# Two pairs of heads per turning transfer, and a new order of the work, in a linear attention with a maxout feed-forward layer

## The chip, the cores and the metric

The kernel runs on one core of a Trainium2 chip. The metric is the device time of one execution in microseconds, and lower is better. Five engines work side by side, each through its own instructions in order: PE (TensorE, matrix products; its loads of weights are listed as PEld), DVE (VectorE), ACT (ScalarE), POOL (GpSimd) and SP (SyncE, which here only issues DMA transfers). Engines wait for each other by semaphores.

## The reference

```
q_s = exp(q - max(q, -1));   q_s /= sum(q_s, -1) + 1e-9      # q, k, v: 8 batches, 8 heads, 576 rows, 64 wide
k_s = exp(k - max(k, 2));    k_s /= sum(k_s, 2) + 1e-9       # over the rows
kv  = einsum('bhsd,bhse->bhde', k_s, v)                      # 64 x 64 for each head
x   = einsum('bhsd,bhde->bhse', q_s, kv) -> (8 * 576, 8 * 64)
h   = maximum(maximum(x @ w1, x @ w2), x @ w3)               # 512 -> 768, float64 weights
out = h @ w_out                                              # 768 -> 512, float32
```

## The kernel before

The unit of the attention is a pair of heads of one batch, since two heads of 64 fill the 128 partitions. Pair n is batch n // 4 and heads 2 (n % 4) and the next; there are 32 pairs. The feed-forward layer runs over chunks of 512 rows, one for each batch, and a ninth of the 8 x 64 rows that are left over. Its products are in two float32r terms each for operand and weights (a high and a low part, three matmuls for one). The weights come as 64-bit words, which `Slice` joins to float32 and splits, 24 slices in all: bits of them are put together by DVE, ACT and POOL (`wx`, `wst`, `wf`), and the parts land in `wa` (three gates, 18 slices) and `oh`, `ol` (second product, six).

The stages: in the first 31 us loads, the first pairs and the first slices; then chunks 0, 1 and 2 by plain products (the gates, L946, and the second product, L993), with the attention of batches 0 to 4 between them; from 292 us on the other six chunks in three "duos" by seven products instead of eight (L1174, of tiles `ws` that SyncE loads back from DRAM copies `keep_a` and `keep_s`), with the attention of batches 5 to 7 between them. Batches 0 and 1 are "turned": PE transposes keys and queries against `ident` (L559, L578, L799). Pair 1's sums are taken by PE after its product (L812, L813), DVE divides (L820), and PE transposes the result (L837, `xr`). The other 24 pairs, n = 8 to 31, are "plain", and the change concerns mostly these:

- keys: loads into `kt` (L515, and L517 for the rows left over), maxima by DVE and POOL, `ksub` (L603), exponentials by ACT (L610); after every second pair `two_products` multiplies the keys' and values' tiles of both (L626), DVE inverts the sums (L632), and ACT and DVE write the head matrices `bdh` and `bdl`, high and low (L639, L647).
- queries: load into `qt` (L548), maximum by DVE (L725), then either nine exponentials with sums by ACT (L729, for n from 8 to 20) or a difference by DVE (L735), one exponential by ACT (L744) and a sum by DVE (L746). The division is by nine ACT instructions (L755, n from 8 to 23) or one of DVE (L760). DVE transposes blocks of 32 into `tb` (L764), and eight DMA transfers (L777) put these blocks in their places in `qT`, which has two rooms.
- query product, `x_steps` (L851): for n from 8 to 16 (`by_f32`) plain float32 matmuls of `qT` with `bdf2`, in two halves; for the others `qT` is split into `q_h` by ACT (L786) and `q_l` by DVE (L789), and six float32r matmuls follow. ACT and DVE copy the result to `x` or `xf`, from where the chunk's products read it.

Nothing of the order is left to the hardware. Generators yield a `Step` for each instruction or small group; `Streams` is a planner that gives every step a cost, due times (`AT`, `FIRST`, `CHUNK`, `PAIR_STEP` and the like set the ranks), rooms of buffers, and picks step by step what each engine does next. Its times are only a plan: on the chip each engine goes through the list that came out, and waits where something is late. SyncE's list matters as the others do: it issues in order, at most eight transfers are open at a time, and a transfer that waits holds up those behind it.

Of the kernel before, what the change touches and what calls it, by code (L numbers as in the profile page):

```python
# [8 lines left out]
F32 = mybir.dt.float32  # L9
# [17 lines left out]
DMA_BEGINS, DMA_LANDS, DMA_EACH, DMA_KB, DMA_LANES = 0.25, 1.3, 0.0095, 0.0375, 8  # L27
DMA_MORE = 1.2
WAIT = 0.02

COLD = 34.0, 1.85

EAGER = 0.21

FIRST, CHUNK, SLICE = 115.59, 38.94, 2.04

PAIR_STEP, LATE_STEP = 7.34, 0.49

AT = (236.9, -68.4, 25.0, -23.0, 44.8, 76.9, 350.7, 199.3)
STEP = (0, 1.04)  # L40
SLICES_AT, SLICE_STEP, SLICE_HI, SLICE_LO = -80.12, -0.08, -2.09, -1.75
GATES_AT = 1000.0
FIRST_LOADS = 'vkwkKqvVwkwqKVqvkvwq'
# [4 lines left out]
Q_BY_ACT = (0, 3, 4, 5, 7)  # L48
# [15 lines left out]
LEFT_AT, KEEP_AT, PLAIN_AT, MIX_AT, MIX_STEP = 149.21, 133.44, 71.96, 363.56, -36.84  # L64
# [26 lines left out]
class Step:  # L91
# [3 lines left out]
    def __init__(self, engine, cost, after=(), gives=None, take=(), free=(), port="", kb=None, rank=None):  # L95
        self.engine, self.gives, self.take, self.free, self.port, self.kb = engine, gives, take, free, port, kb
        self.cost = cost if isinstance(cost, tuple) else (cost,) * len(engine)
        self.after, self.rank = after, rank


class Streams:
# [123 lines left out]
def linear_attention_then_maxout_ffn(  # L225
# [91 lines left out]
    tb = place("tb", [P, 2, BL * QS], F32, SCR_AT + 4608)  # L317
    half = place("kh", [P, 2, 2, D], F32, SCR_AT + 6912)
# [14 lines left out]
    kbuf = [const.tile([P, 2, 5, D], F32, name=f"kt{i}") for i in range(2)]  # L333
    vbuf = [const.tile([P, 2, 5, NV], F32, name=f"vt{i}") for i in range(2)]
    bdh, bdl, bdf2 = [], [], []
# [49 lines left out]
    st = Streams({"pf": 4, "pa": BANKS[0], "sm": BANKS[1], "keT": 1, "hp": NJ, "tmp": 3, "ke": 2, "kep": 1, "qe": 2, "qf": 1, "qt": 2, "tb": 1, "qT": 2, "qhl": 1, "wf": 4, "ws": len(ws), "hs": 2}, {"pf": in_pf, "ws": in_ws, "tb": list(range(TURNED * NP, B * NP))})  # L385
    turn_pools = []

# [87 lines left out]
    class Pair:  # L475
# [30 lines left out]
        def k_load(self):  # L506
            if self.b:
                prev = self.ago("ksub") if self.n >= NP + 2 else None
                if self.turned:
                    for hh in range(2):  # L510
                        yield Step("S", 0.65, [prev], kb=(512, 256))
                        nc.sync.dma_start(out=self.kt[:, 0:4, hh, :], in_=head_rows(k, self.b, 2 * self.g + hh))
                else:
                    yield Step("S", 0.5, [prev], kb=(256, 1024))
                    nc.sync.dma_start(out=self.kt[:, :, 0:4, :], in_=main_rows(k, self.b, self.hs))  # L515
                yield Step("S", 0.69, gives=("k", self.n), kb=(128, 256))
                nc.sync.dma_start(  # L517
                    out=self.kt[0:LEFT, 4] if self.turned else self.kt[0:LEFT, :, 4, :], in_=left_rows(k, self.b, self.hs)
                )

        def v_load(self):
            if self.b:
# [5 lines left out]
                for hh in range(2):  # L528
                    e = yield Step("S" if self.turned else V_ON, 0.5 if self.turned else 0.63, [prev], kb=(128, 1024) if self.turned else (512, 256))
                    if not self.turned:  # L530
                        self.vt = vbuf[self.n % 4]
                    (nc.sync if e == "S" else nc.scalar).dma_start(out=self.vt[:, hh, 0:4, 0:D], in_=head_rows(v, self.b, 2 * self.g + hh))
                yield Step("S", 0.68, gives=("v", self.n), kb=(128, 256))
# [3 lines left out]
        def q_load(self):  # L537
# [7 lines left out]
            else:  # L545
                yield Step("S", 0.5, ["wo"], gives=("q", self.n), take=[("qt", self.n)], kb=(128, 2304))
# [39 lines left out]
        def k_plain(self):  # L586
            n, kt = self.n, self.kt
            yield Step("V", dve(256) + dve(128) * 2, ["turn", ("k", n), ("kmt", n - 1) if n > TURNED * NP else None], port="V")
# [10 lines left out]
            if n % 2:  # L599
                ke = self.ke = turn_pools[0].tile([P, 5, 2, D], F32, name="kep", bufs=1)  # L600
            else:
                ke = self.ke = att.tile([P, 5, 2, D], F32, name="ke")
# [11 lines left out]
        def two_products(self):  # L614
# [5 lines left out]
                free=[("ke", n - 1), ("kep", n)], gives=("kv", n),  # L620
# [13 lines left out]
            for i, p in enumerate(both):  # L634
                fine = by_f32(p.n)
                last = [] if i == 0 else room
                yield Step("A", 0.65, gives=("bd", p.n) if fine else None, free=last if fine else ())
                for r in heads:
                    nc.scalar.activation(  # L639
                        out=(bdf2 if fine else bdh)[p.m][r, r], in_=kv[r, i * P : i * P + D], func=AF.Copy,  # L640
                        scale=rk[r, i : i + 1],
                    )
                if fine:
                    continue
# [39 lines left out]
        def q_steps(self):  # L684
# [79 lines left out]
            nc.vector.transpose(  # L764
                out=tb.rearrange("p e (c s) -> p s e c", s=QS), in_=self.qt.rearrange("p s (e c) -> p s e c", e=2)
            )
            for i in range(P // BL):
                for e in range(2):
                    end = i == P // BL - 1 and e == 1
                    eng = yield Step(  # L770
                        TB_ON, 0.6, ["turn"], take=[("qT", n)] if i == e == 0 else (), free=[("tb", n)] if end else (),
                        gives=("qhl" if by_f32(n) else "qT", n) if end else None, kb=(32, 1152),
                    )
# [3 lines left out]
                    (nc.sync if eng == "S" else nc.scalar).dma_start(  # L777
                        out=self.qT[r : r + BL, BL * QS * (i % 2) : BL * QS * (i % 2 + 1)],
                        in_=tb[BL * i : BL * (i + 1), e, :],
                    )  # L780
# [5 lines left out]
            nc.scalar.copy(out=q_h, in_=self.qT)  # L786
            yield Step("V", dve(S), free=[("qT", n)], gives=("qhl", n), port="V")
            q_l = turn_pools[0].tile([P, S], F32R, name="q_l", bufs=1)
# [35 lines left out]
        def x_steps(self):  # L824
# [3 lines left out]
            fine = by_f32(n)  # L828
# [4 lines left out]
            yield Step("T", cost, after, take=[room] if self.turned else [room, small], gives=("xmm", n), free=[] if after_sums else [freed])  # L833
# [46 lines left out]
    def left_queries():  # L880
# [24 lines left out]
        yield Step("T", 0.5, take=room, free=[("qt", "left")])  # L905
# [5 lines left out]
        yield Step("A", act(CH), take=[("qT", "left")], free=room)  # L911
        qT = turn_pools[0].tile([P, S], F32, name="qT", bufs=2)
# [121 lines left out]
    def keep_weights():  # L1034
# [3 lines left out]
        for i in range(3):  # L1038
            for c in range(NC):
                e = yield Step(  # L1040
                    KEEP_ON, 0.6, [last, *(("split", 3 * j + i) for j in range(NJ))], gives=("kept", i, c), kb=(128, 6144)
                )
                (nc.sync if e == "S" else nc.scalar).dma_start(out=keep_a[i][:, c], in_=wa[i][:, c].bitcast(F32))
# [274 lines left out]
    def open_turn():  # L1318
# [6 lines left out]
        for i in range(4):  # L1325
            nc.gpsimd.memset(vbuf[i][:, :, :, D:NV], 1.0)
            nc.gpsimd.memset(vbuf[i][LEFT:P, :, 4, :], 0.0)
        mixes.append(turn_pools[0].tile([P, 2, NC, 2, P], F32, name="mix"))
        for name, to in (("bdf", bdf2), ("bdh", bdh), ("bdl", bdl)):
            for i in range(2):  # L1330
                to.append(turn_pools[0].tile([P, P], F32 if name == "bdf" else F32R, name=f"{name}{i}"))
# [43 lines left out]
    for (b, g), p in pairs.items():  # L1375
# [11 lines left out]
        st.add(p.q_steps(), at + 0.2, step)  # L1387
        if p.turned:
# [64 lines left out]
```

## Time and profile before

| what | value |
|---|---|
| median of three runs | 680.42 us (680.39 to 680.74) |
| the profiled execution | 681.24 us, its span 679.5 us |
| PE, DVE, ACT, POOL busy | 641.8, 441.0, 365.1, 57.4 us |
| mean granted clock of PE | 0.994 |
| DMA | 135.97 MB in 148534 packets |

The span runs from the first to the last instruction. Busy time is the time in which an engine has an instruction in work. In the rows of waits, the engine that waited and the tile and line that it waited with stand ahead of the arrow, and what came last behind it. "SPq" is SyncE's queue of DMA issues: the time there is that of the issue, not of the transfer. Line numbers in rows of the profile are those of the kernel before; in the changed kernel L777 is L781, L851 is L857, L837 is L843, L626 is L624, L755 is gone.

### The profile page before, as it was taken

Reading aid. Unit: us, or ns where it says so; the run is one execution under the profiler, and the core shown is the slowest. Engines: PE = TensorE matmul, PEld = TensorE weight load, DVE = VectorE, ACT = ScalarE, POOL = GpSimd, SP = SyncE. Lnnn points to the kernel's source line nnn. Section 1 sums busy time; section 2 is a strip of 40 time slices with the busy share of each in tenths; the row PEclk is TensorE's granted clock in tenths of the full one; section 3 lists DMA queues with packets and bytes.
Section 4 is the critical chain, followed back from the end, with each engine's and each line's share of the span. In section 5 each row is a group of like instructions: output and inputs, shape, how many; then the busy total and the mean of one; then the engine's idle time right before and its main releaser. Section 6 shows DMA issues by size and latency. Waiting matters only on the chain.

```text
span 679.5 us, 10529 instructions
## 1 busy us (share of the span) xinstructions
PE 641.8 (94%) x3362; PEld 516.9 (76%) x3362; DVE 441.0 (65%) x830; ACT 365.1 (54%) x1031; POOL 57.4 (8%) x74
## 2 busy tenths in 40 slices
PE   2799999999999899899999999999999999999997
PEld 1587877777777677788888777777888788888875
DVE  6999999476845767997767889945335912333521
ACT  5889759636898786684624365633233532123132
POOL 2232344110000001000000010000000000000000
PEclk9989999999999999999999999999999999999999
DMA  9969587876566667899998756465665126666121
GB/s 234 327 200 326 179 263 238 293 228 157 148 180 172 199 195 201 250 284 322 298 320 259 219 158 173 150 181 174 198 190 173 75 84 194 190 198 189 60 63 62
DMA packets 148534, 135.97 MB, mean 200 GB/s; under 512 B 52992, under 2 KB 120064, under 8 KB 147328
## 3 DMA queue, kind: packets, MB, share of 16 engines
q1 hardware_dynamic: 148400, 135.18, 65.7%
q8 instruction: 27, 0.44, 0.3%
q14 instruction: 27, 0.22, 0.1%
q10 hardware_dynamic: 80, 0.13, 0.1%
HBM read 95.16 MB, written 33.03 MB: 189 GB/s over the span
## 4 chain that ended last, share of the span: by engine, by line
PE 70%; DMA 11%; DVE 8%; SPq 6%; issue 2%; ACT 2%; POOL 0%; DVEq 0%; ACTq 0%
PE pf L1174 33%; PE pf L993 15%; PE pf L946 14%; SPq L777 4%; DMA qt<-in_q_dram 3%; DMA qT<-tb 2%; PE pa L851 2%; DMA bdf<-keep_w 2%; PE pa L626 1%; DMA ws<-keep_s 1%; DMA kt<-in_k_dram 1%; DMA keep_a<-wa 1%; DVE tb L764 1%; PE sm L851 1%; DMA wst<-in_moe_w_dram 1%
## 5 line engine op out<-in xcount | busy, mean ns | idle before, releaser
L1174 PE MATMUL pf<-xb,ws 128*128 128x512 f32 x1134 | 261.8, 390 | 3.2 <-DVE mm L1203 1.4
L1174 PEld LDWEIGHTS pf<-xb,ws 128*128 128x128 f32 x1134 | 211.6, 188 | 48.7 <-ACT pf L1222 2.1
L946 PE MATMUL pf<-x,wa 128*128 128x512 f32 x648 | 159.7, 400 | 1.1 <-DVE x L861 1.1
L946 PEld LDWEIGHTS pf<-x,wa 128*128 128x128 f32 x648 | 120.4, 189 | 28.7 <-DVE x L861 1.7
L993 PE MATMUL pf<-oh,hs 128*128 128x512 f32 x288 | 89.9, 391 | 0.3 <-DVE hs L1258 0.3
L1203 DVE TENSOR_TENSOR mm<-pf,mm 128x512 f32<-128x512 f32 x36 | 24.9, 690 | 76.3 <-PE pf L1174 76.2
L993 PEld LDWEIGHTS pf<-oh,hs 128*128 128x128 f32 x288 | 54.1, 188 | 12.9 <-DVE hs L1258 2.0
L1222 ACT COPY pf<-pf 128x512 f32<-128x512 f32 x27 | 15.4, 571 | 80.6 <-PE pf L1174 80.6
L993 PE MATMUL pf<-ol,hs 128*128 128x512 f32 x144 | 56.5, 392 | 0.0
L755 ACT ACTIVATE qt<-qt,qs 128x64 f32<-128x64 f32 x144 | 38.4, 339 | 14.1 <-DVE qs L749 14.0
L729 ACT ACTIVATE qt<-qt,qm 128x64 f32<-128x64 f32 x117 | 39.4, 340 | 10.2 <-DVE qm L725 10.1
L1258 DVE TENSOR_TENSOR hs<-mm,hs 128x512 fp32r<-128x512 f32 (+1 forms) x48 | 25.8, 562 | 29.0 <-ACT hs L1256 28.9
L1019 ACT COPY m<-pf 128x512 f32<-128x512 f32 x35 | 20.3, 585 | 41.3 <-PE pf L993 40.0
L596 POOL PARTITION_ALL_REDUCE kma<-km x24 | 18.7, 781 | 272.1 <-DVE km L593 143.6
L764 DVE STREAM_TRANSPOSE tb<-qt 128x576 f32<-128x576 f32 x24 | 30.7, 1278 | 14.9 <-DMA qT<-tb 5.2
L993 PEld LDWEIGHTS pf<-ol,hs 128*128 128x128 f32 x144 | 27.0, 188 | 6.0 <-ACT hs L1256 0.5
L1215 ACT COPY u<-pf 128x512 f32<-128x512 f32 x27 | 15.8, 586 | 27.1 <-PE pf L1174 27.1
L440 POOL TENSOR_TENSOR wf<-wx,wst 128x512 int32<-128x512 int32 x18 | 24.8, 1379 | 62.8 <-DVE wx L431 26.9
L993 PE MATMUL pf<-ol,h_h 128*128 128x512 f32 x72 | 29.3, 407 | 0.0
L725 DVE TENSOR_REDUCE qm<-qt 128x9 f32<-128x576 f32 x24 | 17.8, 744 | 16.2 <-DMA qt<-in_q_dram 16.0
L993 PE MATMUL pf<-oh,h_l 128*128 128x512 f32 x72 | 28.1, 390 | 0.0
L993 PE MATMUL pf<-oh,h_h 128*128 128x512 f32 x72 | 28.0, 389 | 0.0
(188 smaller groups left out, 906.8 us busy)
## 6 DMA issues: line engine op xcount, KB each, us to landing
ws<-keep_s SPq DMA_DIRECT2D x108, 256.0 KB, 3.2
ws<-keep_a SPq DMA_DIRECT2D x81, 256.0 KB, 3.2
wst<-in_moe_w_dram SPq DMA_DIRECT2D x18, 512.0 KB, 5.3
keep_a<-wa SPq DMA_DIRECT2D x12, 768.0 KB, 5.6
keep_s<-mix SPq DMA_DIRECT2D x9, 1024.0 KB, 5.8
out_dram<-m SPq DMA_DIRECT2D x31, 256.0 KB, 2.2
vt<-in_v_dram SPq DMA_DIRECT2D x56, 128.0 KB, 3.1
qt<-in_q_dram SPq DMA_DIRECT2D x24, 288.0 KB, 3.3
```

Source lines behind the costliest of these rows:

```text
L440: nc.gpsimd.tensor_add(out=self.w.bitcast(I32), in0=x.bitcast(I32), in1=low.bitcast(I32))
L729: nc.scalar.activation(out=rows3[:, s, :], in_=rows3[:, s, :], func=AF.Exp, bias=qm[:, s : s + 1], accum_out=qs[:, s : s + 1],)
L755: nc.scalar.activation(out=rows3[:, s, :], in_=rows3[:, s, :], func=AF.Copy, scale=qs[:, s : s + 1])
L764: nc.vector.transpose(out=tb.rearrange("p e (c s) -> p s e c", s=QS), in_=self.qt.rearrange("p s (e c) -> p s e c", e=2))
L777: (nc.sync if eng == "S" else nc.scalar).dma_start(out=self.qT[r : r + BL, BL * QS * (i % 2) : BL * QS * (i % 2 + 1)], in_=tb[BL * i : BL ...
L851: nc.tensor.matmul(out=out, lhsT=l, rhs=r[:, cs], start=(i == 0), stop=(i == last))
L946: nc.tensor.matmul(out=ps, lhsT=l[:, cc, js], rhs=r, start=(cc == 0 and t == 0), stop=(cc == NC - 1 and t == 2))
L993: nc.tensor.matmul(out=po, lhsT=l, rhs=r[:, j, :], start=(j == 0 and i == 0), stop=(j == NJ - 1 and i == 2))
L1019: nc.scalar.copy(out=o, in_=po)
L1174: nc.tensor.matmul(out=bank[on], lhsT=w[:, k, a], rhs=x[:, b, k], start=(i == 0 and p in ("P1", "P5")), stop=(i == 5), skip_group_check=True,)
L1203: nc.vector.tensor_max(out=m, in0=bank[on], in1=m)
L1258: nc.vector.tensor_tensor(out=o[:, 1, jj], in0=mm[:, h, jj, ts], in1=o[:, 0, jj].bitcast(F32), op=ALU.subtract)
```

## The change

Three things change.

1. Plain keys are loaded for two pairs at once: `kboth` holds both, one load of 512 KB waits for the `ksub` of the last pair of the two before. `tb` holds two pairs, each of the eight turning transfers carries both (64 runs of 1152 bytes for 32), and `qT` is one room for two pairs where it was two rooms for one. So `q_l` is written over `qT`, and splitting the queries is a stream of its own, `q_terms`. A room is free again when the second pair's product is done.
2. `by_f32` and `bdf2` go: every plain pair is multiplied in six matmuls of halves.
3. The planner: `Step` has a `slack` that is added to the time from which a step may begin, 2.0 for the products of sums and the query products of plain pairs; costs of SyncE's steps are other numbers; all due times, the order of the first loads and who does what are new. No plain division is on ACT any more (`NORM_TO` 24 to 8), and four more pairs take exponentials with sums on ACT (`ROWS_TO` 21 to 25). Of the turned pairs, 3, 4 and 6 take theirs on ACT, where 0, 3, 4, 5 and 7 did.

```diff
-DMA_BEGINS, DMA_LANDS, DMA_EACH, DMA_KB, DMA_LANES = 0.25, 1.3, 0.0095, 0.0375, 8
+DMA_BEGINS, DMA_LANDS, DMA_EACH, DMA_KB, DMA_LANES = 0.25, 1.4, 0.0095, 0.0375, 8
+SLACK = 2.0
...
-AT = (236.9, -68.4, 25.0, -23.0, 44.8, 76.9, 350.7, 199.3)
+AT = (85.0, -48.0, 27.5, 32.6, 191.4, 127.7, 214.6, 44.9)
...
-FIRST_LOADS = 'vkwkKqvVwkwqKVqvkvwq'
+FIRST_LOADS = 'kvwvKkqwwVKVkqkqqwwvv'
...
-Q_BY_ACT = (0, 3, 4, 5, 7)
+Q_BY_ACT = (3, 4, 6)
-NORM_FROM, NORM_TO = 8, 24
-F32_FROM, F32_TO = 8, 17
-ROWS_FROM, ROWS_TO = 8, 21
+NORM_FROM, NORM_TO = 8, 8
+ROWS_FROM, ROWS_TO = 8, 25
...
-        lat = SIGNAL + (AHEAD if engine == "T" else 0.0)
+        lat = SIGNAL + (AHEAD if engine == "T" else 0.0) + step.slack
...
-    kbuf = [const.tile([P, 2, 5, D], F32, name=f"kt{i}") for i in range(2)]
+    kboth = const.tile([P, 4, 5, D], F32, name="kt")
+    kbuf = [kboth[:, 2 * i : 2 * i + 2] for i in range(2)]
...
-                    yield Step("S", 0.5, [prev], kb=(256, 1024))
-                    nc.sync.dma_start(out=self.kt[:, :, 0:4, :], in_=main_rows(k, self.b, self.hs))
+                elif self.m == 0:
+                    hs = slice(2 * self.g, 2 * self.g + 4)
+                    yield Step("S", 0.62, [prev, ("ksub", self.n - 1)], kb=(512, 1024))
+                    nc.sync.dma_start(out=kboth[:, :, 0:4, :], in_=main_rows(k, self.b, hs))
+                    yield Step("S", 0.71, gives=("k", self.n), kb=(256, 256))
+                    nc.sync.dma_start(out=kboth[0:LEFT, :, 4, :], in_=left_rows(k, self.b, hs))
...
-            yield Step("V", dve(2 * rows * D), take=[("tb", n)], free=[("qt", n)])
+            both = n - self.m
+            yield Step(
+                "V", dve(2 * rows * D), [("tb", n - 1) if self.m else "turn"], take=() if self.m else [("tb", both)],
+                free=[("qt", n)], gives=("tb", n),
+            )
...
+            if not self.m:
+                return
             for i in range(P // BL):
                 for e in range(2):
...
-                        self.qT = turn_pools[0].tile([P, S], F32, name="qT", bufs=2)
+                        qT = turn_pools[0].tile([P, 2, S], F32, name="qT", bufs=1)
+                        for p in (pairs[divmod(both, NP)], self):
+                            p.qT = qT[:, p.m]
...
-                        in_=tb[BL * i : BL * (i + 1), e, :],
+                        in_=tb[BL * i : BL * (i + 1), :, e, :],
...
-            if by_f32(n):
-                self.terms = [(bdf2[self.m], self.qT)]
-                return
-            yield Step("A", act(S), [("qT", n)], take=[("qhl", n)])
+        def q_terms(self):
+            n = self.n
+            both = n - self.m
+            yield Step("A", act(S), [("qT", both)], take=[("qhl", n)])
             q_h = turn_pools[0].tile([P, S], F32R, name="q_h", bufs=1)
             nc.scalar.copy(out=q_h, in_=self.qT)
...
-            q_l = turn_pools[0].tile([P, S], F32R, name="q_l", bufs=1)
+            q_l = self.qT.bitcast(F32R)
...
-            cost = 0.5 if after_sums else f32(CH) if self.turned else 4 * f32r(S) if fine else 6 * f32r(S // 2)
-            freed = ("qf" if self.turned else "qT" if fine else "qhl", n)
+            cost = 0.5 if after_sums else f32(CH) if self.turned else 6 * f32r(S // 2)
+            freed = [("qf" if self.turned else "qhl", n)]
+            if not self.turned and self.m:
+                freed.append(("qT", n - 1))
```

Three places of the order. First PE at the start, around pair 1's sums (`of_head`): before, the first product of a gate (`wa_78`) stands ahead of the sums:

```order
L946 MATMUL pf<-x_81,wa_78 128x512 x3
L669 MATMUL pf<-v_165,ke 64x64 x10
L812 MATMUL pf<-of_head,qf 128x2
L813 MATMUL pa<-bdf,qf 128x128
L812 MATMUL pf<-of_head,qf 128x2
L813 MATMUL pa<-bdf,qf 128x128
L812 MATMUL pf<-of_head,qf 128x2
L813 MATMUL pa<-bdf,qf 128x128
L812 MATMUL pf<-of_head,qf 128x2
L813 MATMUL pa<-bdf,qf 128x128
L799 MATMUL pa<-ident,qe 128x128 x4
L946 MATMUL pf<-x_81,wa_79 128x512 x3
```

In the changed kernel it stands behind them:

```order
L817 MATMUL pf<-of_head,qf 128x2
L818 MATMUL pa<-bdf,qf 128x128
L664 MATMUL pf<-v_164,ke 64x64 x10
L804 MATMUL pa<-ident,qe 128x128 x4
L952 MATMUL pf<-x_81,wa_78 128x512 x3
L576 MATMUL pa<-ident,keT 128x128 x4
L577 MATMUL pf<-ident,keT 64x128
L952 MATMUL pf<-x_81,wa_79 128x512 x3
```

The first gate's product moved behind the sums, a third product of keys and values and a third transpose of queries.

Second, SyncE in the middle of the attention of plain pairs. Before, between the turning transfers of two single pairs:

```order
L515 DMA kt_159<-in_k_dram 128x2x256
L517 DMA kt_159<-in_k_dram 64x2x64
L777 DMA qT<-tb 32x288 x8
L548 DMA qt_110<-in_q_dram 128x576
L548 DMA qt_111<-in_q_dram 128x576
L777 DMA qT<-tb 32x288 x8
L532 DMA vt_161<-in_v_dram 128x4x64 x2
L535 DMA vt_161<-in_v_dram 64x2x64
L515 DMA kt_160<-in_k_dram 128x2x256
L517 DMA kt_160<-in_k_dram 64x2x64
```

Now, with eight transfers for two pairs and one load of keys:

```order
L781 DMA qT<-tb 32x2x288 x8
L530 DMA vt_1435<-in_v_dram 128x4x64
L1079 DMA keep_s_147<-mix 128x2048
L1063 DMA bdf<-keep_w_139 128x1024
L515 DMA kt<-in_k_dram 128x4x256
L517 DMA kt<-in_k_dram 64x4x64
L530 DMA vt_1434<-in_v_dram 128x4x64 x2
L546 DMA qt_111<-in_q_dram 128x576
L533 DMA vt_1434<-in_v_dram 64x2x64
L530 DMA vt_1435<-in_v_dram 128x4x64
L533 DMA vt_1435<-in_v_dram 64x2x64
```

Half of the turning transfers and of the loads of keys are gone from the queue.

Third, PE from a product of sums (`ke`, `kep`) to the next query product. Before, the first such place:

```order
L626 MATMUL pa<-vt_161,ke 64x65 x10
L626 MATMUL pa<-vt_162,kep 64x65 x10
L946 MATMUL pf<-x_82,wa_79 128x512 x12
L851 MATMUL pa<-qT,bdf_1539 128x288
L851 MATMUL sm<-qT,bdf_1539 128x288
```

Now the second such place, which is one of the shortest turns from a second pair's product to the next pair's:

```order
L952 MATMUL pf<-x_82,wa_78 128x512 x3
L952 MATMUL pf<-x_82,wa_79 128x512 x12
L624 MATMUL pa<-vt_1434,ke 64x65 x10
L624 MATMUL pa<-vt_1435,kep 64x65 x10
L952 MATMUL pf<-x_82,wa_80 128x512 x12
L952 MATMUL pf<-x_82,wa_78 128x512 x12
L952 MATMUL pf<-x_82,wa_79 128x512 x12
L952 MATMUL pf<-x_82,wa_80 128x512 x3
L857 MATMUL pa<-qT,bdh_1448 128x288
L857 MATMUL sm<-qT,bdh_1448 128x288
```

The query product moved from 12 matmuls behind the sums to 39, and the query's matmuls read the halves' matrices `bdh`.

More of the change, by code (lines that the diff above doesn't have):

```diff
@@ L91, with __init__ @@
 class Step:
-    def __init__(self, engine, cost, after=(), gives=None, take=(), free=(), port="", kb=None, rank=None):
+    def __init__(self, engine, cost, after=(), gives=None, take=(), free=(), port="", kb=None, rank=None, slack=0.0):
         self.engine, self.gives, self.take, self.free, self.port, self.kb = engine, gives, take, free, port, kb
         self.cost = cost if isinstance(cost, tuple) else (cost,) * len(engine)
-        self.after, self.rank = after, rank
+        self.after, self.rank, self.slack = after, rank, slack
 class Streams:
@@ L316, in linear_attention_then_maxout_ffn @@
     qts = Placed("qt", [P, QS, D], F32, SCR_AT, 2)
-    tb = place("tb", [P, 2, BL * QS], F32, SCR_AT + 4608)
-    half = place("kh", [P, 2, 2, D], F32, SCR_AT + 6912)
+    half = place("kh", [P, 2, 2, D], F32, SCR_AT + 4608)
+    kep = place("kep", [P, 5, 2, D], F32, SCR_AT + 5632)
     mixes = []
@@ L384, in linear_attention_then_maxout_ffn @@
         in_pf += [("S", c, i) for i in range(4)] + [(c, "y", t) for t in range(8)]
[L385 removed]
+    st = Streams({"pf": 4, "pa": BANKS[0], "sm": BANKS[1], "keT": 1, "hp": NJ, "tmp": 3, "ke": 2, "kep": 1, "qe": 2, "qf": 1, "qt": 2, "tb": 1, "qT": 1, "qhl": 1, "wf": 4, "ws": len(ws), "hs": 2}, {"pf": in_pf, "ws": in_ws, "tb": list(range(TURNED * NP, B * NP, 2))})
     turn_pools = []
+    tb = None
     class Slice:
@@ L599, in k_plain @@
             if n % 2:
-                ke = self.ke = turn_pools[0].tile([P, 5, 2, D], F32, name="kep", bufs=1)
+                ke = self.ke = kep
             else:
@@ L619, in two_products @@
                 "T", 1.4, [("v", n - 1), ("v", n), ("kexp", n - 1), self.ago("xmm", 3), self.ago("xmm")], take=room,
-                free=[("ke", n - 1), ("kep", n)], gives=("kv", n),
+                free=[("ke", n - 1), ("kep", n)], gives=("kv", n), slack=SLACK,
             )
@@ L634, in two_products @@
             for i, p in enumerate(both):
-                fine = by_f32(p.n)
                 last = [] if i == 0 else room
-                yield Step("A", 0.65, gives=("bd", p.n) if fine else None, free=last if fine else ())
+                yield Step("A", 0.65)
                 for r in heads:
                     nc.scalar.activation(
-                        out=(bdf2 if fine else bdh)[p.m][r, r], in_=kv[r, i * P : i * P + D], func=AF.Copy,
+                        out=bdh[p.m][r, r], in_=kv[r, i * P : i * P + D], func=AF.Copy,
                         scale=rk[r, i : i + 1],
                     )
-                if fine:
-                    continue
                 yield Step("V", 0.45, gives=("bd", p.n), free=last)
@@ L827, in x_steps @@
             after_sums = self.turned and n in Q_AFTER
-            fine = by_f32(n)
-            cost = 0.5 if after_sums else f32(CH) if self.turned else 4 * f32r(S) if fine else 6 * f32r(S // 2)
-            freed = ("qf" if self.turned else "qT" if fine else "qhl", n)
+            cost = 0.5 if after_sums else f32(CH) if self.turned else 6 * f32r(S // 2)
+            freed = [("qf" if self.turned else "qhl", n)]
+            if not self.turned and self.m:
+                freed.append(("qT", n - 1))
             after = [("bd", n), ("qhl", n), x_free(b), "late" if b == 1 else None]
             small = ("sm", n)
-            yield Step("T", cost, after, take=[room] if self.turned else [room, small], gives=("xmm", n), free=[] if after_sums else [freed])
+            yield Step("T", cost, after, take=[room] if self.turned else [room, small], gives=("xmm", n), free=[] if after_sums else freed, slack=0.0 if self.turned else SLACK)
             xT = pa.tile([P, CH], F32, name="pa")
@@ L904, in left_queries @@
         room = [("pa", ("qT", "left"))]
-        yield Step("T", 0.5, take=room, free=[("qt", "left")])
+        yield Step("T", 0.5, take=[*room, ("qT", "left")], free=[("qt", "left")])
         qTp = pa.tile([P, CH], F32, name="pa")
@@ L910, in left_queries @@
             )
-        yield Step("A", act(CH), take=[("qT", "left")], free=room)
-        qT = turn_pools[0].tile([P, S], F32, name="qT", bufs=2)
+        yield Step("A", act(CH), free=room)
+        qT = turn_pools[0].tile([P, 2, S], F32, name="qT", bufs=1)[:, 0]
         nc.scalar.copy(out=qT[:, :CH], in_=qTp)
@@ L1039, in keep_weights @@
             for c in range(NC):
-                e = yield Step(
-                    KEEP_ON, 0.6, [last, *(("split", 3 * j + i) for j in range(NJ))], gives=("kept", i, c), kb=(128, 6144)
+                yield Step(
+                    "S", 0.6, [last, *(("split", 3 * j + i) for j in range(NJ))], gives=("kept", i, c), kb=(128, 6144)
                 )
-                (nc.sync if e == "S" else nc.scalar).dma_start(out=keep_a[i][:, c], in_=wa[i][:, c].bitcast(F32))
+                nc.sync.dma_start(out=keep_a[i][:, c], in_=wa[i][:, c].bitcast(F32))
                 last = ("kept", i, c)
@@ L1327, in open_turn @@
             nc.gpsimd.memset(vbuf[i][LEFT:P, :, 4, :], 0.0)
+        nonlocal tb
+        tb = turn_pools[0].tile([P, 2, 2, BL * QS], F32, name="tb")
         mixes.append(turn_pools[0].tile([P, 2, NC, 2, P], F32, name="mix"))
-        for name, to in (("bdf", bdf2), ("bdh", bdh), ("bdl", bdl)):
+        for name, to in (("bdh", bdh), ("bdl", bdl)):
             for i in range(2):
-                to.append(turn_pools[0].tile([P, P], F32 if name == "bdf" else F32R, name=f"{name}{i}"))
+                to.append(turn_pools[0].tile([P, P], F32R, name=f"{name}{i}"))
                 nc.gpsimd.memset(to[i].bitcast(F32), 0.0)
@@ L1387, in linear_attention_then_maxout_ffn @@
         st.add(p.q_steps(), at + 0.2, step)
+        if not p.turned:
+            st.add(p.q_terms(), at + 0.2 + 8 * step, step)
         if p.turned:
```

52 lines of the change are left out of this document (24 added, 28 removed).

## The prediction

> **What bounds the kernel now.** I read the page's busy times first, then the span cut at 31, 145, 280, 380 and 480 us, then the waits of PE, and then SyncE's queue (SPq). The page:
>
> ```profile
> span 679.5 us, 10529 instructions
> PE 641.8 (94%) x3362; PEld 516.9 (76%) x3362; DVE 441.0 (65%) x830; ACT 365.1 (54%) x1031; POOL 57.4 (8%) x74
> ```
>
> PE is the bound: 679.5 - 641.8 = 37.7 us are all that it does not work. The stretches (first the stretch, then its length, then each engine's busy time) say where these lie:
>
> ```profile
> 0.00:31.00 31.00, 14.64 (x86) 9.78 (x86) 24.89 (x63) 19.89 (x61) 7.42 (x13) 1.00 1.03 281
> 31.00:145.00 114.00, 113.79 (x639) 90.86 (x640) 95.11 (x195) 86.77 (x269) 33.40 (x41) 0.97 0.77 249
> 145.00:280.00 135.00, 124.32 (x748) 98.48 (x747) 92.52 (x189) 101.09 (x384) 9.44 (x13) 1.00 0.65 187
> 280.00:380.00 100.00, 100.00 (x517) 82.44 (x516) 80.81 (x147) 52.71 (x118) 3.17 (x4) 1.00 0.93 287
> 380.00:480.00 100.00, 94.07 (x521) 75.22 (x520) 73.72 (x128) 47.47 (x100) 4.00 (x4) 1.00 0.59 175
> 480.00:679.50 199.50, 195.02 (x857) 160.16 (x855) 74.00 (x111) 57.12 (x103) 0.00 (x0) 1.00 0.45 138
> ```
>
> PE is idle for 16.4 us at the start, 10.7 us from 145 to 280, 5.9 us from 380 to 480, and 4.5 us at the end, where the last tile is copied and written, which the change leaves alone. The waits of PE (releaser, us in total, times, longest):
>
> ```profile
> PE pa L578 <- ACT keT L572: 7.6, 3, 5.1
> PE pa L559 <- DMA k<-in_k_dram: 6.0, 1, 6.0
> PE pa L851 <- DVE q_l L789: 5.8, 8, 2.0
> PE pa L851 <- ACT qt L729: 2.3, 1, 2.3
> ...
> PE sm L851 <- ACT qt L755: 1.4, 2, 0.7
> ...
> PE sm L851 <- ACT qt L729: 1.3, 1, 1.3
> ...
> PE sm L851 <- ACT kep L610: 1.3, 1, 1.3
> ```
>
> The first two lie at the start. Of the 16.6 us in the two middle stretches, the rows of L851, the query products, make 12.1: PE has no lack of other work there, it stands in its order at a product whose query has not come. Why it has not come shows in SyncE's queue, which turns the queries by DMA (L777):
>
> ```profile
> 173.88 5.01 SPq L777 DMA_DIRECT2D qT<-tb  x8
> 178.99 3.22 SPq L548 DMA_DIRECT2D qt<-in_q_dram  x2
> 182.31 5.43 SPq L777 DMA_DIRECT2D qT<-tb  x8
> 187.84 1.32 SPq L532 DMA_DIRECT2D vt<-in_v_dram  x2
> ```
>
> The issues follow each other without a gap: the queue is full, and every query waits its turn in it.
>
> **The change, term by term.**
>
> *SyncE's queue.* The three lines that get fewer (min/median/max ns of one issue) and the landing of L777's transfers, in us:
>
> ```profile
> L777 SPq DMA_DIRECT2D qT<-tb x192: 507/588/2527, 129.2 to 465.8; - x192
> DMA to landing us min/median/max: 1.8/3.0/7.9
> L515 SPq DMA_DIRECT2D kt<-in_k_dram x24: 379/540/588, 79.7 to 411.6; - x24
> L517 SPq DMA_DIRECT2D kt<-in_k_dram x28: 607/627/1621, 22.8 to 412.3; - x28
> ```
>
> The new order has 96 transposing transfers of two pairs for 192 of one, and for the plain batches 12 key loads and 12 rests of two pairs for 24 and 24. An issue that moves twice the rows is not in the trace; L515 and L517 differ by a factor of eight in bytes and cost 0.54 and 0.63, so I take an unchanged price. Freed: 96 x 0.588 + 12 x 0.540 + 12 x 0.627 = 70.4 us of queue, about half of it between 145 and 280, where half of the pairs are turned. By the Trainium skill's page "DMA: Bandwidth & Descriptors", section "Anatomy of one DMA — SWDGE (gpsimd) path", the sequencer spends some 50 ns on a DMA (told there for GpSimd's path); by that figure 120 issues would free 6 us, which is next to nothing, and the sum would be that of the second rival below. The row of L777, ten times as long, does not agree for SyncE's queue.
>
> *DVE and ACT.* The rows (count | busy us, mean ns):
>
> ```profile
> L755 ACT ACTIVATE qt<-qt,qs 128x64 f32<-128x64 f32 x144 | 38.4, 339 | 14.1 <-DVE qs L749 14.0
> L729 ACT ACTIVATE qt<-qt,qm 128x64 f32<-128x64 f32 x117 | 39.4, 340 | 10.2 <-DVE qm L725 10.1
> L786 ACT CAST q_h<-qT 128x576 fp32r<-128x576 f32 x15 | 10.1, 675 | 16.0 <-DMA qT<-tb 10.0 <-DMA ws<-keep_s 6.0
> L789 DVE TENSOR_TENSOR q_l<-qT,q_h 128x576 fp32r<-128x576 f32 x15 | 11.3, 751 | 2.6 <-DMA ws<-keep_s 1.8 <-ACT q_h L786 0.7
> L760 DVE TENSOR_TENSOR qt<-qt,qs 128x576 f32<-128x576 f32 x8 | 6.0, 752 | 0.1
> ```
>
> ACT loses all 144 of L755 (38.4 us) and gains 36 of L729 (36 x 0.34 = 12.2) and 9 of L786 (6.1): 20 us less. DVE gains 16 of L760 and 9 of L789, 25 x 0.75 = 18.8 us, and 18 small low parts of the head matrices; four pairs whose exponential goes to ACT give back 8 x 0.75 = 6. This hides: from 145 to 280 DVE is busy for 92.5 of 135 us and would be at some 110. Without that cover each pair would cost up to its 1.5 us more, late at its product.
>
> *PE's own work.* Nine pairs change from four plain matmuls to six in halves:
>
> ```profile
> 146.14 0.65 PE L851 MATMUL pa<-qT,bdf 128*128 128x288 f32 x2
> 146.62 0.65 PE L851 MATMUL sm<-qT,bdf 128*128 128x288 f32 x2
> 146.89 4.50 PE L946 MATMUL pf<-x,wa 128*128 128x512 f32 x18
> ...
> 435.84 0.29 PE L851 MATMUL pa<-q_l,bdh 128*128 128x288 f32 x1
> ...
> 436.63 0.62 PE L1174 MATMUL pf<-xb,ws 128*128 128x512 f32 x2
> ```
>
> Amid other work the plain product holds PE from 146.14 to 146.89, 0.75 us, and the halves from 435.84 to 436.63, 0.79 us. Nine times 0.04 is 0.4; single products scatter by 0.15, so 0, between -1.5 and +1.5.
>
> *Products planned later.* Counted in the two orders, from a product of sums (L626) to the next query product stand 12, 24, 21, 18, 36, 24 and 81 big matmuls before and 24, 39, 60, 39, 39, 45 and 66 now, each some 0.23 us (below). The head matrix and the query get 2.8 to 9 us more in five of seven places, 0.7 in one, and in the last 66 matmuls remain; the waits of L851 were at most 2.3 us. With a queue that is no longer full, I take it that three quarters of the 12.1 us go: -9.1. The rows of L1174, L993 and L946 keep theirs: each duo still starts soon after its last queries (the second one 36 matmuls after them for 57), so nothing is won there. Bounds: 0, and -16.6 with every wait of the middle gone.
>
> *The start.* The loads stand in another order. Up to the first keys' rest both orders load 1.25 MB (the weights' slice, keys and values); then the first query, which came at once, now comes behind two more loads of keys. DVE works for 24.9 of the first 31 us. In the new order DVE does less ahead of the division that PE waits for at L837: one slice of weights less (L424, L426, L427, L431 and L455 once less each), one L760 and two divisions (two small instructions each) less, one L716 and one L746 more, which read as many elements as L760.
>
> ```profile
> 8.43 0.43 DVE L427 TENSOR_SCALAR wx<-wx 128x512 uint32<-128x512 uint32 x1
> 8.89 0.69 DVE L431 SCALAR_TENSOR_TENSOR wx<-wst,wx 128x512 uint32<-128x512 uint32 x1
> ...
> 35.33 0.17 DVE L748 TENSOR_SCALAR qs<-qs 128x8 f32<-128x8 f32 x1
> 35.53 0.20 DVE L749 RECIPROCAL qs<-qs 128x8 f32<-128x8 f32 x1
> ```
>
> Three of 0.43 (L424 has the size of L426 and L427), three of 0.69 less two of 0.69, and twice 0.37 make 2.7 us less. Since the first query lands later, I take -2.0; between -5 (a third of the 16.4 us) and +3 (the wait of 6.0 for the first keys grown by half).
>
> *The sum.* -9.1 - 2.0 + 0 = -11.1. The profiled execution took 681.24 (its span 679.5 and 1.7 around it): 670.1. The median of the runs shown, 680.42, is 0.8 lower, so 669.3.
>
> **Rivals.**
>
> *The single room makes a turn (slower).* The turned queries have one room of two pairs for two of one. The next eight transfers leave only after PE's second product of the two, so a turn runs through SyncE, DMA, ACT and DVE before PE's next product. For it: eight issues 5.0 (row at 173.88), landing 3.0, L786 0.68, L789 0.75 and about 0.3 for signals: 9.7 us. The shortest turns of the new order hold 54 matmuls and one product of sums:
>
> ```profile
> 236.78 10.26 PE pf L946 x45
> ...
> 276.27 1.32 PE pa L626 x40
> ...
> 226.41 8.25 SPq L777 DMA_DIRECT2D qT<-tb  x8
> ```
>
> 54 x 10.26 / 45 + 1.32 = 13.6 us, so 3.9 us are to spare in each of the six turns that are this short (four of 54, two of 60). It turns when a transfer stands behind an issue that itself waits, as in the row at 226.41 (3.2 us longer), and lands at the slowest 7.9: 9.7 + 3.2 + 4.9 = 17.8, 4.2 us late, six times: 25 us, 694. The gain is gone from 11.1 / 6 = 1.9 us late on average. Against it: only a median transfer is needed, and the queue is emptier. The same page of the Trainium skill, section "Rules for kernel authors", says to issue a DMA early and to wait late, so that its fixed time is covered; the one room does the opposite, and by that rule this rival is the outcome. No row of this trace has such a turn.
>
> *The queue was not the limit (no gain in the middle).* The releasers of L851 are DVE and ACT; if their own order made the products late, the waits only move. Then the start alone counts: 680.4 - 2.0 = 678.4, or 680.4 without it. Against it: the full queue.
>
> *The start goes the other way.* +3 for -2: 674.3. For it speaks the later first query and values.
>
> *All waits of the middle go.* 680.4 - 16.6 - 2.0 = 661.8, which takes that the duos' starts no longer wait.
>
> **How the numbers follow.** My forecast, with its own range of 665 to 674, has 0.52; the turn 0.12; no gain in the middle 0.12 (a third of it within 0.2%, which is about what a measurement of this kernel can tell from no change); the start 0.13; all waits gone 0.11. Faster: 0.52 + 0.08 + 0.13 + 0.11 = 0.84; within 0.2%: 0.04; slower: 0.12. The range 662 to 682 leaves out most of the turn and part of the last case, less than 0.2.
>
> **What would show it.** Right: 96 issues of `qT<-tb` at about 0.6 us; gaps in SyncE's queue between 160 and 235; the waits of PE at the query products (now L857) summing to 3 us or less; the division's transposes (now L843) at about 37 us for 39.4. Wrong: an issue of a double transfer near 1.2 us; waits of PE of 2 us and more at every other query product, released by DVE's low part behind a DMA; PE idle for over 18 us before 31 us, or a new wait at the duos' starts, where 36 matmuls now cover what 57 did.

## The result, and the profile after

The changed kernel takes 662.48 us (662.11 to 662.89, four runs), the kernel before 680.4 us in the same session. The ratio is 0.9741, with an interval of 0.9724 to 0.9758: 17.9 us less, where 11.1 were forecast. The time lies below my own range of 665 to 674 and only half a microsecond inside the outer one of 662 to 682. The page and the six stretches of the profiled execution (length, then busy time of PE, weight loads, DVE, ACT, POOL):

```profile
span 660.5 us, 10328 instructions
PE 633.7 (96%) x3380; PEld 516.8 (78%) x3380; DVE 461.3 (70%) x863; ACT 344.9 (52%) x939; POOL 59.2 (9%) x73
```

```profile
0.00:31.00 31.00, 16.11 (x101) 11.52 (x101) 26.26 (x61) 18.45 (x48) 7.53 (x13) 1.00 1.01 277
31.00:145.00 114.00, 107.32 (x604) 82.39 (x602) 102.48 (x196) 81.97 (x244) 34.60 (x38) 0.99 0.75 237
145.00:280.00 135.00, 134.30 (x837) 112.07 (x832) 117.46 (x244) 92.48 (x328) 11.43 (x14) 1.00 0.76 223
280.00:380.00 100.00, 100.00 (x521) 83.19 (x520) 78.77 (x148) 51.92 (x129) 2.84 (x4) 1.00 0.93 287
380.00:480.00 100.00, 100.00 (x560) 83.27 (x559) 71.09 (x122) 47.04 (x98) 2.84 (x4) 1.00 0.60 177
```

From 145 to 280 us PE starts 837 matmuls where it started 748, and from 380 to 480 us 560 where it started 521. From 31 to 145 us it starts fewer, 604 for 639: something was lost there. The waits of PE that are left (releaser, us in total, times, longest):

```profile
PE pa L557 <- DMA k<-in_k_dram: 4.8, 1, 4.8
PE pf L560 <- DMA k<-in_k_dram: 3.2, 2, 2.9
PE pa L576 <- ACT keT L570: 3.1, 1, 3.1
PE pa L804 <- DVE x L867: 1.8, 1, 1.8
PE pa L857 <- ACT qf L808: 1.6, 1, 1.6
...
PE pf L999 <- DVE ol L452: 1.1, 1, 1.1
...
PE pf L999 <- DVE h_l L971: 0.7, 1, 0.7
```

Behind 145 us only the last row is left. The one row of L857 is a turned pair's (`qf`); no plain query product waits.

**Where the time went.** Idle time in the records is less than what a stop costs: a matmul is recorded for 0.39 us while the next starts after 0.23, so a wait swallows 0.16 us before it shows. I therefore took the time from each matmul's start to the next, less the median of its kind over both traces, and call the rest lost. For a plain product by f32 I took 0.75 us, which it takes where nothing holds it up (two of nine before, eight of nine in e6 below), since their median before, 0.98, is itself full of waits; one by halves takes 0.79. In us:

| | before | after | difference |
|---|---|---|---|
| first matmul begins at | 6.0 | 4.8 | -1.3 |
| lost from there to 31 us | 15.5 | 14.5 | -0.9 |
| lost, 31 to 145 | 7.5 | 14.8 | +7.3 |
| lost, 145 to 280 | 18.5 | 3.5 | -14.9 |
| lost, 280 to 380 | 1.2 | 0.7 | -0.4 |
| lost, from 380 on | 10.9 | 1.8 | -9.1 |
| PE's own work | 615.1 | 615.5 | +0.4 |
| sum, to the last matmul | 674.6 | 655.6 | -19.0 |

Of the 24.5 us won from 145 us on, some 18 lay at the plain query products (all 24 take 0.79 us now, and none begins late) and 4.5 in the duos.

### The profile page after: what moved, and what is told of

Read it like the earlier page. It is cut to its first block, busy times and chain, and to the rows that moved or that the text cites. A ratio compares the mean times of both kernels' runs of the same rounds, so it can differ in the third digit from the quotient of the medians.

```text
span 660.5 us, 10328 instructions
## 1 busy us (share of the span) xinstructions
PE 633.7 (96%) x3380; PEld 516.8 (78%) x3380; DVE 461.3 (70%) x863; ACT 344.9 (52%) x939; POOL 59.2 (9%) x73
## 4 chain that ended last, share of the span: by engine, by line
PE 80%; DVE 9%; ACT 3%; DMA 2%; issue 1%; SPq 1%; DVEq 0%; ACTq 0%
PE pf L1180 39%; PE pf L999 20%; PE pf L952 16%; PE pa L624 2%; PE pa L857 2%; PE sm L857 1%; DVE wx L428 1%; DVE wx L423 1%; DVE wa L452 1%; DMA bdf<-keep_w 1%; DVE wx L424 1%; DVE qe L755 1%; DMA wst<-in_moe_w_out_dram 1%; ACT qt L724 1%; DVE m L964 1%
## 5 line engine op out<-in xcount | busy, mean ns | idle before, releaser
L1180 PE MATMUL pf<-xb,ws 128*128 128x512 f32 x1134 | 260.4, 390 | 0.0
L1180 PEld LDWEIGHTS pf<-xb,ws 128*128 128x128 f32 x1134 | 212.2, 188 | 43.9
L952 PE MATMUL pf<-x,wa 128*128 128x512 f32 x648 | 156.7, 395 | 0.0
L724 ACT ACTIVATE qt<-qt,qm 128x64 f32<-128x64 f32 x153 | 51.3, 338 | 4.2 <-DVE qm L720 3.8
L437 POOL TENSOR_TENSOR wf<-wx,wst 128x512 int32<-128x512 int32 x18 | 26.4, 1467 | 56.4 <-DVE wx L428 38.9
L724 ACT ACTIVATION_READ_ACCUMULATOR qt<-qt,qm 128x1 f32 x153 | 28.9, 189 | 0.0
L1262 ACT CAST hs<-mm 128x512 fp32r<-128x512 f32 (+1 forms) x48 | 23.1, 513 | 8.9 <-DVE mm L1216 8.9
```

What stands on the lines that cost most here:

```text
L437: nc.gpsimd.tensor_add(out=self.w.bitcast(I32), in0=x.bitcast(I32), in1=low.bitcast(I32))
L724: nc.scalar.activation(out=rows3[:, s, :], in_=rows3[:, s, :], func=AF.Exp, bias=qm[:, s : s + 1], accum_out=qs[:, s : s + 1],)
L952: nc.tensor.matmul(out=ps, lhsT=l[:, cc, js], rhs=r, start=(cc == 0 and t == 0), stop=(cc == NC - 1 and t == 2))
L1180: nc.tensor.matmul(out=bank[on], lhsT=w[:, k, a], rhs=x[:, b, k], start=(i == 0 and p in ("P1", "P5")), stop=(i == 5), skip_group_check=True,)
L1262: nc.scalar.copy(out=o[:, 0, jj], in_=mm[:, h, jj, ts])
```

## The experiments

Medians are beside the kernel before on the same chip (678.1 to 679.6). A planner that gets another number writes another order from that place on, so a run tells of one number only if the trace shows the mechanism too.

**e1: twice the issues, the same order.**

```diff
-nc.sync.dma_start(out=qT[r : r + BL, :, ...], in_=tb[BL * i : BL * (i + 1), :, e, :])
+for m in range(2):
+    nc.sync.dma_start(out=qT[r : r + BL, m, ...], in_=tb[BL * i : BL * (i + 1), m, e, :])
```

> The changed kernel with every turning transfer of two pairs issued as two transfers of one pair each (192 issues again, the same bytes, the same order on every engine). Theory Q (the waits at the query products went because SyncE's queue got 96 issues fewer): 96 x 0.59 = 57 us come back into the queue, half of it between 145 and 280 us, and at least half of the 12 us of waits at the query products come back: 668 to 676. Theory L (the waits went because the plan puts sums and query products later): the order is the same and has 2 us in hand at each product: 662 to 664.5.

705.0 us (ratio 1.0377, 1.0332 to 1.0423), far more than theory Q gave. A turn is now sixteen issues, and ACT waits 38.0 us for the queries, for 1.5 in the changed kernel (first a row of SyncE's queue, then one of ACT's waits, then the stretch from 145 to 280 us):

```profile
224.06 11.04 SPq L782 DMA_DIRECT2D qT<-tb  x16
```

```profile
ACT q_h L792 <- DMA qT<-tb: 38.0, 11, 5.2
```

```profile
145.00:280.00 135.00, 122.88 (x748) 99.43 (x747) 98.04 (x207) 77.95 (x287) 9.20 (x12) 0.97 0.63 190
```

748 matmuls in that stretch, as many as in the kernel before. Theory L falls: with 2 us in hand at each product the order does not stand 192 issues. The plan knew nothing of the 96 more issues, here and in e11, so both runs tell what this order loses by them; e8 below shows an order that was planned with 192.

**e11: the issues, but not the long turn.**

```diff
+if end:
+    for m in range(8):
+        nc.sync.dma_start(out=idle[4 * both + m], in_=ident[0:BL, :])
```

> The changed kernel with eight small idle transfers (32 rows of 512 B, to a scratch tensor that nobody reads) behind the eight turning transfers of every two pairs, so that SyncE's queue has 96 issues more, as in e1 (705.0), but a turn is still eight issues and the room is handed over as fast as in the change. Theory F (the full queue as such makes everything behind it late): some 50 us of issues more, most of e1's 42 us come back: 690 to 708. Theory R (e1 was slow because a turn of sixteen issues through the one room took 4.7 us longer than the plan left for it, and the rest of the queue has slack): 662.5 to 672.

691.65 us (1.0167, 1.0125 to 1.0209). SyncE's queue behind one turn:

```profile
194.47 4.35 SPq L782 DMA_DIRECT2D qT<-tb  x6
198.86 3.83 SPq L788 DMA_DIRECT2D idle<-ident  x8
202.79 0.40 SPq L516 DMA_DIRECT2D kt<-in_k_dram  x1
```

The issues of SyncE, summed over the records, took 351.6 us, for 298.4 in the changed kernel: 53 us of queue cost 29 us of time, while the eight issues of a turn take as long as in the changed kernel (a median of 6.7 us from first to last, for 11.4 in e1). So some 29 of e1's 42.5 us come with more issues alone; that the other 13 go with the longer turn is what is left, and was not tested by itself. Both theories hold a part, F the larger.

**e2: no slack.** `SLACK = 2.0` becomes `0.0`.

> The changed kernel planned with SLACK 0 for 2.0: sums and query products of the plain pairs stand where the planner believes that they are just ready. The first 175 rows of PE stay. Theory Q: the queue is as free as before, the waits stay away: 661.5 to 665. Theory L: the margin is gone and waits of some 0.5 us return at most of the 24 query products and 12 sums: 668 to 676, with over 6 us of waits at the query products in the trace.

664.95 us (0.9792, 0.975 to 0.9833), 2.5 us more than the change. One wait of 0.6 us at a plain query product is back:

```profile
PE pf L1180 <- ACT mm L1206: 0.6, 1, 0.6
PE pa L857 <- DVE qT L794: 0.6, 1, 0.6
```

Theory Q holds: where the queue is free, the slack is worth little. But the run tells of the slack alone. Its query products stand no nearer to the sums: 18, 24, 75, 48, 75, 48 and 87 big matmuls behind them at the first seven places, for 24, 39, 60, 39, 39, 45 and 66 in the change.

**e3: the slack alone, in the kernel before.** `slack=2.0` on L626's and L851's steps.

> The kernel before with nothing changed but 2.0 us of slack on plain sums and query products in the plan (192 issues, plain products by f32, every other number of before). Theory Q: the full queue still makes the queries late: 676 to 682. Theory L: most of the 12.1 us at the query products and of the waits of the second products go: 666 to 672.

675.51 us (0.994, 0.9916 to 0.9965): it lies below theory Q's interval by half a microsecond and far above theory L's. The loss at the query products fell from about 18 to under 8 us, but the second products now wait, where 0.3 us had been:

```profile
PE pf L993 <- ACT hs L1256: 1.9, 1, 1.9
PE pf L993 <- DVE h_l L965: 1.9, 2, 1.1
PE pf L993 <- DVE hs L1258: 1.4, 2, 0.8
```

**e4: pairs and halves, with the numbers of before** (due times, loads, who divides, `SLACK` 0).

> The changed kernel with all numbers of the plan as before (due times, loads, slack 0, who divides, whose rows on ACT); only paired transfers, the in-place low part, all products in halves and SyncE's new costs are left of the change. Theory Q: the queue is freed as in the change, and the middle's gain is there: 664 to 672. Theory L: without slack the waits stay: 676 to 682.

677.35 us (0.9962, 0.9942 to 0.9982): by the total theory L, by the trace neither. Two stretches, and a wait of PE:

```profile
145.00:280.00 135.00, 135.00 (x868) 112.89 (x867) 103.64 (x215) 112.48 (x414) 8.80 (x12) 1.00 0.66 199
280.00:380.00 100.00, 91.40 (x460) 74.80 (x460) 84.02 (x160) 51.19 (x113) 4.28 (x6) 0.95 0.95 291
```

```profile
PE pa L857 <- DVE qT L794: 9.2, 4, 4.2
```

From 145 to 280 us pairing brings the whole gain without any slack (PE is never idle). From 280 to 380 us it is given back (14.5 us lost, 1.2 before, 0.7 in the change): that stretch is nearly all of what e4 takes more than the change. There a turn through the one room is cut in two by what stands between its issues in SyncE's list:

```profile
332.35 4.05 SPq L781 DMA_DIRECT2D qT<-tb  x5
...
342.18 0.38 SPq L1151 DMA_DIRECT2D ws<-keep_a  x1
342.62 1.89 SPq L781 DMA_DIRECT2D qT<-tb  x3
```

Five transfers leave at 332.35, the last three ten microseconds later, behind seven loads of `ws`, ahead of which SyncE waits for other transfers to land (3.0 us in its records). PE then waits 1.1 us for that pair's queries, and, with no big matmul planned between, 3.3 us for the next pair's. The next turn is cut as well (two issues at 361.76, six from 365.75), and PE waits 4.2 us for it.

**e9: e4 with the slack.**

> The run e4 (paired transfers and halves, all due times of before) with 2.0 us of slack on plain sums and query products. In e4 the stretch from 145 to 280 us lost only 2.8 us of PE's time and the one from 280 to 380 lost 14.5, at three products whose turn through the one room was late by 1.1 to 4.2 us. If slack is what makes room for the turn: those three waits go, 664 to 669. If the due times decide (where a pair's load, its turn and the next products stand against each other): the late turns stay or move, 672 to 682.

686.09 us (1.0107, 1.0085 to 1.0129), worse than both theories. The stretch from 145 to 280 us stays full, and the late turn is dearer:

```profile
PE pa L857 <- DVE qT L794: 10.4, 2, 5.7
```

**e8: the new due times, first loads and turned exponentials in the kernel before.**

> The kernel before with the changed kernel's due times, first loads and choice of turned exponentials, and nothing else: 192 issues, plain products by f32, divisions on ACT, no slack. With the run that had paired transfers and the due times of before (677.4), it makes the other half of a square. Theory Q+N (the pairing's gain between 145 and 280 us needs the new due times to survive later, and the due times alone have a full queue): 674 to 690. Theory N (the due times alone are the gain): 662 to 668.

705.1 us (1.0367, 1.0308 to 1.0425). Theory N falls, and the loss is larger than Q+N gave. The four corners:

| | numbers of before | new numbers |
|---|---|---|
| 192 turning issues | 679.6 | 705.1 (e8) |
| 96 turning issues | 677.4 (e4) | 665.0 (e2), with slack 662.5 |

The pairs alone gain 2 us, the new numbers alone lose 26. In the right column e2 also has the divisions on DVE and more exponentials on ACT, which e8 has not.

**e12: one room in the kernel before.** `bufs=2` of `qT` becomes `bufs=1`.

> The kernel before with one room for the turned queries (bufs 1 for 2) and nothing else, planned anew: every pair's eight transfers leave only after PE's product of the pair ahead. Theory R (one room makes a turn that PE waits for): a turn of 9.7 us stands 24 times, and between the two products of a duo's pairs PE had 12 to 60 big matmuls (2.8 to 14 us); half of the turns some 2 us short, 24 us: 695 to 710. Theory F (the queue is what is late, the room hardly counts): 678 to 686.

684.85 us (1.0084, 1.0052 to 1.0115), within theory F. One room cost some 6 us there. In the changed kernel it can't be seen as a cost at all, since no product waits; two rooms of two pairs were not tried.

**e6: f32 for nine pairs in the changed kernel.** `F32_FROM, F32_TO = 8, 17` with `bdf2` again.

> The changed kernel with the plain products of pairs 8 to 16 by f32 again (four matmuls for six, no high and low parts of query and head matrix for them), planned anew. Start to start in the traces the four take 0.66 us and the six 0.79. If the halves cost PE 0.13 us each and nothing else: nine times, 1.2 us less, 660 to 662.5. If the halves are part of the gain (the f32 products of before were the ones that waited): 665 to 672. If DVE and ACT, which lose 9 x 0.75 and 9 x 0.68 us and 9 low parts, were limits: below 660.

667.88 us (0.9821, 0.9774 to 0.9868). The number is that of the second theory, but the trace denies it: the nine f32 products begin on time, and eight of them take 0.75 us (so 0.04 less than by halves, not the 0.13 of the expectation, whose 0.66 is no time from start to start). The 5 us lie at other places (the start, the first chunks' second products, the end of a duo) and go with the new order.

**e7: divisions on ACT again.** `NORM_TO` 8 becomes 24.

> The changed kernel with the divisions of 16 plain pairs on ACT again (144 small instructions of 0.34 us, 49 us; DVE 16 x 0.75 = 12 us less), planned anew. Theory A (ACT's chain of nine small instructions made the queries late, and its removal is a part of the middle's gain): 667 to 678, with waits at the query products of over 5 us between 145 and 280. Theory Q (only SyncE's queue counted): 661.5 to 665.

668.59 us (0.9835, 0.9785 to 0.9885). The number is theory A's, the mechanism is not: from 145 to 280 us only 2.0 us are lost, and the waits have moved to the duos (L1180, 6.2 us lost), where ACT and DVE are late with the parts of `x`:

```profile
PE pf L1180 <- DVE xb L1113: 1.9, 2, 1.3
```

**e5 and e10: the loss between 31 and 145 us.** `Q_BY_ACT` (3, 4, 6) becomes (0, 3, 4, 5, 7) and (3, 4, 5, 7).

> The changed kernel with the exponentials of the turned queries as before: five pairs with their sums on ACT (0, 3, 4, 5, 7) for three. Between 31 and 145 us the changed kernel lost 7.3 us more of PE's time than the kernel before, and DVE was busy there for 102.5 of 114 us for 95.1. Theory D (DVE is the limit there, and the two pairs moved to it are the cause): two times a subtraction and a sum, 2 x (0.69 + 0.68) = 2.7 us of DVE less, and the early loss shrinks by 2 to 4: 658 to 660.5. Theory S (the early loss is the scatter of one order among many): no shift that follows DVE's work, 660.5 to 666.

> The changed kernel with the exponentials of turned pairs 3, 4, 5 and 7 on ACT for 3, 4 and 6, so that the first pairs stay as they are (in e5 pair 0 moved as well, and PE then waited 11.1 us for ACT's copies of the first keys). Theory D (between 31 and 145 us DVE is the limit): one pair less on DVE, 0.69 + 0.68 = 1.4 us, and the loss of PE's time in that stretch, 14.8 us in the changed kernel, shrinks by 1 to 3: 659.5 to 661.5. Theory S (scatter of the order): 661.5 to 666, the loss not smaller.

676.72 us (0.9955, 0.993 to 0.9981) and 664.08 us (0.978, 0.9754 to 0.9805). Neither reduced the early loss (22.9 and 16.3 us for 14.8). In e5 pair 0's exponentials stand ahead of ACT's copies of the first keys:

```profile
PE pa L576 <- ACT keT L570: 11.1, 4, 3.6
```

The times that theory D gave did not come, and e5 lies above both theories. But DVE was not relieved there either: it is busy for 104.8 and 103.5 us of that stretch, for 102.5 in the changed kernel, since the planner put other work in the place of what left. So these runs neither show nor refute DVE as the cause; what the trace of the change says of it stands in the next section.

## Why the prediction was right or wrong

**SyncE's queue: right, and the main cause.** An issue of twice the bytes costs the same, and the queue has gaps:

```profile
L781 SPq DMA_DIRECT2D qT<-tb x96: 585/595/2199, 128.8 to 436.8; - x96
```

```profile
171.11 0.60 SPq L1049 DMA_DIRECT2D keep_a<-wa  x1
180.63 0.83 SPq L546 DMA_DIRECT2D qt<-in_q_dram  x2
184.43 1.31 SPq L781 DMA_DIRECT2D qT<-tb  x2
```

A median of 0.595 for 0.588 us; 9 us without an issue from 171.7. All issues took 298.4 us for 378.4, 80 freed where 70.4 were forecast, and 29 of them from 145 to 280 us where I put half. "Full" was too strong for the whole stretch: SyncE issued for 114.6 of its 135 us before and for 85.7 now. e1 and e11 show that the freed issues were needed, e4 that with them PE is never idle from 145 to 280 us even without slack and with the old due times. What the loads of keys for two pairs add by themselves was not tested.

**Products planned later: the term that was mis-sized.** I took three quarters of the 12.1 us of recorded waits, -9.1; the stretches from 145 us on gave -24.5. Three things were short. The recorded waits understate the loss: some 18 us lay at these products. All of it went. And the duos' waits, which I kept, went too (`L1174 <- DVE mm` and its like: 3.2 us before, none after). Even my bound of -16.6 was taken from idle time and so was too small. The reason is in part open: I credited the later products. (Place for place the first goes from 12 matmuls to 24 and the second from 24 to 39; the 12 and the 39 that are compared ahead of the prediction are different places.) That lateness isn't enough is shown: e1 and e11 have exactly the change's distances and lose 19 and 13 us at the plain query products. Whether it is needed no run shows, since e2, which takes only the slack, 2.5 us, leaves the products as late. From 280 us on, what let the freed queue count is the new numbers as a whole (e4 against e2); in e4's trace it is where turns stand against the loads of `ws`.

**The stretch from 31 to 145 us: a term that I left out.** I gave it nothing, since PE was hardly idle there; it lost 7.3 us more. Most of it can be placed: between 109 and 121 us the changed kernel loses 5.4 us, the kernel before next to nothing. The rows of a late piece of the second product's weights:

```profile
106.37 0.68 DVE L452 TENSOR_TENSOR ol<-wst,oh 128x512 fp32r<-128x512 f32 x1
107.08 0.33 SPq L409 DMA_DIRECT2D wst<-in_moe_w_out_dram  x1
111.54 0.66 ACT L441 ACTIVATE wst<-wst 128x512 int32<-128x512 uint32 x1 [2.20 <-DMA wst<-in_moe_w_out_dram]
112.72 1.44 PE L857 MATMUL pa<-qf,bdf 128*128 128x512 f32 x2 [1.56 <-ACT qf L808]
```

DVE, busy for 9.9 us of the 10 before, writes the low part of the slice before only at 106.37, though both of its inputs were written by 101.23; that frees a room of `wst`. The load that waits for the room lands 4.4 us after its issue; ACT stands for 2.2 us at it, with the copy of a turned pair's query (`qf`, L808) behind it in its list, and PE waits 1.6 us for that copy. A window at half the clock follows (last section), and 1.1 us for the next slice. So at this place the chain leads back to DVE's list; no run took work off DVE there, so it is read from one trace and not shown by an experiment, and the other 2 us stay open. What I could have seen is that DVE was busy there for 95 of 114 us, with work to be added: I asked whether that hides only from 145 to 280 us.

**The start: right in size.** -2.2 us for -2.0. The division's transposes are at 34.9 us for 39.39 (37 forecast), so that mark was passed by 2 us, and part of it is another reason than mine: the first keys are loaded first, and the first matmul begins 1.3 us earlier.

**PE's own work: right.** 0.79 us for each product by halves, 0.75 for one by f32; nine times 0.04 is the +0.4 of the table.

**DVE and ACT hidden: right from 145 us on.** DVE is busy for 117.5 of 135 us there, where I said some 110.

**The rivals.** By the time, "all waits of the middle go" came true (661.8 forecast), but by luck: as a larger gain less a loss that it didn't have. No product waited for the turn through the one room in this order. It is real all the same: it took back the gain in e4 and e9, and e1 showed what a turn of sixteen issues does. "Queue not the limit" is refuted by e1 and e11. By the Trainium skill's page "DMA: Bandwidth & Descriptors", section "Anatomy of one DMA — SWDGE (gpsimd) path", 120 fewer issues at some 50 ns would be 6 us of queue, an estimate from a figure told for GpSimd's path; 80 us were measured, so for SyncE's queue the trace does not agree.

## What to carry to other kernels

Where every engine follows a written order, count the issues on the DMA queue first. Here the same bytes in half the issues freed what the new order alone did not, and the order made for the freed queue was worse than the old one without it. Measure a lost wait from start to start and not by idle time. A stretch whose bound engine is never idle can still lose in a new order: before giving it no term, look at how full the second engine is.

## What the hardware showed unexpectedly

A stop of PE can cost more than itself, because the granted clock may halve after it. Three windows of the changed kernel, then three of the kernel before, then three of e9 (PE's busy time is the second number, the granted clock the third from the end):

```profile
110.00:113.41 3.41, 1.51 (x8) 0.87 (x7) 3.41 (x6) 1.87 (x7) 0.00 (x0) 1.00 0.71 292
113.41:116.82 3.41, 3.41 (x9) 2.33 (x8) 3.31 (x6) 2.51 (x11) 1.31 (x2) 0.50 0.82 231
116.82:120.24 3.42, 2.34 (x10) 1.60 (x10) 2.26 (x7) 3.42 (x15) 1.29 (x1) 1.00 1.02 428
```

```profile
29.66:33.07 3.41, 2.24 (x26) 1.36 (x26) 3.38 (x9) 3.13 (x11) 1.30 (x1) 1.00 1.16 320
33.07:39.89 6.82, 6.82 (x31) 6.39 (x31) 6.38 (x19) 4.59 (x15) 1.30 (x1) 0.50 0.84 244
39.89:43.30 3.41, 3.41 (x34) 2.48 (x32) 2.37 (x6) 3.25 (x15) 0.88 (x1) 1.00 0.61 185
```

```profile
281.18:284.59 3.41, 0.00 (x0) 0.00 (x0) 1.70 (x2) 2.60 (x7) 0.00 (x0) 1.00 1.09 309
284.59:311.90 27.31, 15.68 (x72) 11.68 (x73) 24.47 (x40) 16.89 (x41) 1.77 (x2) 0.50 0.53 158
311.90:315.31 3.41, 3.41 (x16) 2.78 (x16) 2.15 (x3) 0.59 (x3) 0.00 (x0) 1.00 1.01 336
```

The half clock comes in whole windows of 3.41 us. In the fourteen traces, behind 45 us and at the full clock, it followed every window in which PE was idle for 1.88 us or more (3.41 at most), and none with less than 1.68; in between both occurred (1.68 in e11 was enough, 1.85 in e12 was not). In the kernel before, at 29.66 us amid short transposes, 1.2 us were enough. In e9 27.3 us at half the clock went with two late queries of 5.7 and 4.7 us and a late `xb` of 3.9 us that came on top. The Trainium skill's page "TensorE: Matmul & The Clock Gate", section "Part 1: The HAM clock gate", has the same window of about 3.4 us, but lets the clock fall after an idle window; here about half a window of idle time was enough.
